# Reordering loads and the first two attention units, with wider idle matmuls, at the start of a fused attention and MLP kernel

## The chip, the cores and the metric

One core of a Trainium2 chip. The metric is the device time of one execution in microseconds (us), smaller is better. "Profile" is one execution recorded by the hardware profiler; its span (first to last instruction) is about 1.7 us shorter than the time.

## The reference

```python
# q, k, v: (8, 8, 576, 64); attention inside chunks of 64 tokens
scores = scale * q_c @ k_c.T ; attn = softmax(scores) ; x = attn @ v_c
x = x.transpose(0, 2, 1, 3).reshape(4608, 512)
h = x @ w_in                                # 512 -> 2048
g = h * sigmoid(beta * h)
out = g @ w_out                             # 2048 -> 512, float32
```

## The kernel before

The 4608 tokens are taken in units of 256, two units making a block of 512. For each unit: scores on TensorE, exp on ScalarE, PV on TensorE, normalisation on VectorE (a reciprocal and a multiply for each half), a transpose of x on TensorE with a copy to SBUF on ScalarE. For each block: sixteen groups "m" of the hidden layer (in the profile `hps`: four matmuls each, then tanh on ScalarE and a multiply on VectorE into `gt`), then the output layer (`ops`). From the third unit on attention is mixed into the matmuls of the MLP. The first two units cannot be: at the start there is nothing else to compute. Idle matmuls on a zeroed tile fill the waits there.

The loads of q, k, v and the weights go through one queue, issued by GpSimd in program order:

```python
# unit 0: half of q, k by SP into raw0, the other half here into qk0[1]
load_v(0)
load_v(1)
load_qk(1)
load_w_in(0)
load_v(2)
load_v(3)
...
for g in range(1, 8):
    load_w_in(g)
# [... w_out, later units ...]
```

and the computation at the start is

```python
emit_idle(10, 512); emit_idle(4, 128)
emit_T_half(0); emit_sc_half(0)          # scores of unit 0, first half of the heads
emit_idle(14, 128)
emit_T_half(1); emit_sc_half(1)
# [... beta ...]
emit_idle(8, 128)
emit_pv(0); emit_norm(0, 0); emit_norm(0, 1)
emit_idle(10, 128); emit_xt_pe(0, 0)
emit_idle(8, 128);  emit_xt_pe(0, 1)
emit_idle(24, 128)
emit_T(1); emit_sc(1, True)              # scores of unit 1
# m0, m1 for the first 256 tokens, PV of unit 1, norms, emit_idle(8, 128), transposes, m2 ... m5 for the first 256,
# then m0 ... m5 for the second 256, then m6 ... m15 for all 512

def emit_idle(n, w):
    d = ps_p.tile([128, 512], FP32, tag="p", name="warm")
    for _ in range(n):
        nc.tensor.matmul(out=d[:, 0:w], lhsT=idle[:, 0:128], rhs=idle[:, 0:w])
```

The softmax here doesn't subtract the row's maximum and nothing guards it: scores larger than these inputs give would overflow.

## Time and profile before

| | before |
|---|---|
| time, median of the 3 runs known ahead | 291.59 us (291.19 to 291.81) |
| TensorE busy | 282.5 us of a span of 290.3 |
| idle matmuls | 86, 9.9 us |
| scores of unit 1 begin | 13.24 us |
| PV of unit 1 begins | 15.56 us |
| first matmul of the output layer (end of block 0's hidden layer) | 31.09 us |

The best single number is the start of the first output-layer matmul: everything of the front lies ahead of it. I call it "first ops" below. It comes from one profiled execution, and that one took 292.08 us.

### The profile page before, as it was taken

How to read it: one execution, taken by the hardware profiler on the slowest of the kernel's cores; microseconds unless marked ns; L12 is line 12 of the kernel's file. 1: busy time of each engine (PE TensorE's matmuls, PEld its weight loads, DVE VectorE, ACT ScalarE, POOL GpSimd, SP SyncE). 2: the span in 40 equal slices, each digit the busy share in tenths (PEclk: the TensorE clock that was granted, in tenths of full speed). 3: DMA queues.
4: the chain of work that ended last, by engine and by line, in shares of the span. 5: the costliest groups of instructions: out<-in, count | busy, mean ns of one | idle time of the engine just before them, and what ended most of it. 6: DMA issues, size and time to landing. Idle time of an engine off the chain costs nothing.

```text
span 290.3 us, 6592 instructions
## 1 busy us (share of the span) xinstructions
PE 282.5 (97%) x2750; PEld 138.6 (48%) x2750; DVE 139.7 (48%) x254; ACT 146.3 (50%) x227; POOL 97.5 (34%) x126
## 2 busy tenths in 40 slices
PE   8799999999999999999999999999999999999995
PEld 4674445545544444444444444444444444444444
DVE  3467444687266544534454444545353636433300
ACT  3288318783556545454544554455445544444411
POOL 8863668479152985070807070000000000000000
PEclk9999999999999999999999999999999999999999
DMA  9999999999969999999999999524343212001011
GB/s 138 174 196 205 180 181 211 210 157 159 129 98 143 171 180 148 194 143 156 125 160 146 158 108 183 114 71 95 87 105 78 74 37 74 36 36 38 36 72 72
DMA packets 141932, 36.86 MB, mean 127 GB/s; under 512 B 130000, under 2 KB 137424, under 8 KB 141904
## 3 DMA queue, kind: packets, MB, share of 16 engines
q0 software_dynamic: 101216, 18.10, 80.8%
q1 hardware_dynamic: 40544, 18.24, 31.1%
q8 instruction: 21, 0.34, 0.5%
q10 hardware_dynamic: 144, 0.13, 0.1%
q14 instruction: 7, 0.06, 0.1%
HBM read 36.71 MB, written 9.44 MB: 159 GB/s over the span
## 4 chain that ended last, share of the span: by engine, by line
PE 90%; DVE 2%; DMA 2%; POOL 2%; ACT 1%; issue 1%; DVEq 0%; POOLq 0%
PE hps L303 43%; PE ops L335 41%; DMA ku<-in_k_dram 2%; PE x L256 2%; PE sc L231 2%; PE sc L218 1%; PE ops L547 1%; DVE x L271 1%; POOL vbig L110 1%; POOL h L360 1%; PE xp L287 1%; ACT xt L288 1%; ACT sg L313 1%; DVE kT L154 0%; DVE qT L154 0%
## 5 line engine op out<-in xcount | busy, mean ns | idle before, releaser
L317 DVE SCALAR_TENSOR_TENSOR gt<-sg,hps 128x512 f16<-128x512 f32 (+1 forms) x154 | 99.3, 652 | 115.0 <-ACT sg L313 114.8
L313 ACT ACTIVATE sg<-hps,beta 128x512 f32<-128x512 f32 (+1 forms) x154 | 100.6, 660 | 73.8 <-PE hps L303 73.8
L303 PE MATMUL hps<-xt,win 128*128 128x512 f16 (+1 forms) x616 | 136.7, 365 | 0.7 <-issue 0.3
L335 PE MATMUL ops<-wout,gt 128*128 128x512 f16 x560 | 131.1, 379 | 0.0
L303 PEld LDWEIGHTS <-win 128*128 128x128 f16 x616 | 58.3, 98 | 61.5 <-issue 1.5
L335 PEld LDWEIGHTS <-gt 128*128 128x128 f16 x560 | 53.7, 98 | 63.3
L345 ACT ACTIVATE osb<-ops 128x512 f32<-128x512 f32 x35 | 20.9, 598 | 44.3 <-PE ops L335 44.3
L110 POOL DMA_DIRECT2D vbig<-in_v_dram x40 | 34.1, 871 | 11.4 <-DMA wout<-in_moe_w_out_dram 4.3
L96 POOL DMA_DIRECT2D qu<-in_q_dram x22 | 18.7, 863 | 39.8 <-DMA qT<-qu 36.4
L271 DVE TENSOR_TENSOR x<-x,rd 128x512 f16<-128x512 f32 (+1 forms) x40 | 25.2, 637 | 1.4
L96 POOL DMA_DIRECT2D ku<-in_k_dram x22 | 18.8, 876 | 0.0
L240 ACT ACTIVATE et<-sc 128x512 f16<-128x512 f32 (+1 forms) x10 | 7.5, 768 | 10.4 <-PE sc L231 10.3
L267 DVE RECIPROCAL rd<-x 128x8 f32<-128x8 f32 x36 | 7.2, 200 | 10.2 <-PE x L256 10.2
L352 PE MATMUL warm<-idle 128*128 128x128 f16 (+1 forms) x86 | 9.9, 272 | 1.2 <-DVE braw L356 1.2
L224 ACT ACTIVATE et<-sc 128x1024 f16<-128x1024 f32 x10 | 10.2, 1016 | 0.0
L256 PEld LDWEIGHTS <-et 64*64 64x64 f16 x576 | 6.3, 107 | 7.5 <-issue 3.0
L288 ACT COPY xt<-xp 128x512 f16<-128x512 f16 x12 | 6.7, 588 | 4.5 <-PE xp L287 4.5
L256 PE MATMUL x<-vbig,et 64*64 64x65 f16 x576 | 8.6, 195 | 0.3 <-DMA vbig<-in_v_dram 0.3
L102 POOL DMA_DIRECT2D qu<-in_q_dram x10 | 7.8, 789 | 2.4 <-DMA win<-in_moe_w_in_dram 1.4
L102 POOL DMA_DIRECT2D ku<-in_k_dram x10 | 7.7, 768 | 2.4 <-DMA win<-in_moe_w_in_dram 1.3
L352 PEld LDWEIGHTS <-idle 128*128 128x128 f16 x86 | 6.0, 105 | 4.1 <-issue 2.8
L154 DVE STREAM_TRANSPOSE kT<-ku 128x512 f32<-128x512 f32 x7 | 5.0, 711 | 4.4 <-DMA ku<-in_k_dram 4.3
(34 smaller groups left out, 57.1 us busy)
## 6 DMA issues: line engine op xcount, KB each, us to landing
out_dram<-osb SPq DMA_DIRECT2D x35, 256.0 KB, 3.8
vbig<-in_v_dram POOLq DMA_DIRECT2D x32, 128.0 KB, 7.6
qu<-in_q_dram POOLq DMA_DIRECT2D x20, 128.0 KB, 5.5
ku<-in_k_dram POOLq DMA_DIRECT2D x20, 128.0 KB, 7.4
win<-in_moe_w_in_dram POOLq DMA_DIRECT2D x8, 256.0 KB, 8.8
wout<-in_moe_w_out_dram POOLq DMA_DIRECT2D x4, 512.0 KB, 12.2
qu<-in_q_dram POOLq DMA_DIRECT2D x4, 256.0 KB, 6.8
ku<-in_k_dram POOLq DMA_DIRECT2D x4, 256.0 KB, 7.2
```

The source lines that it names most:

```text
L96: nc.gpsimd.dma_start(out=tv[off:off + n, sp], in_=src[b, :, s:s + n, :].rearrange("h p d -> p h d"),)
L102: nc.gpsimd.dma_start(out=t[off // 2:(off + n) // 2], in_=src[b, :, s:s + n, :].rearrange("h (p r) d -> p h r d", r=2),)
L110: nc.gpsimd.dma_start(out=vbig[off:off + n, i, :, 0:D], in_=v[b, :, s:s + n, :].rearrange("h p d -> p h d"),)
L224: nc.scalar.activation(out=et, in_=sc, func=ACTF.Exp, scale=scale)
L256: nc.tensor.matmul(out=x[64 * c:64 * c + 64, r, g, 0:D + 1], lhsT=(et[64 * r:64 * r + 64, s, 4 * c + g, :] if u < XU else et[64 * r:64 * r ...
L271: nc.vector.tensor_tensor(out=o, in0=x[:, r, :, 0:D], in1=rd[:, r].to_broadcast(list(o.shape)), op=ALU.mult)
L303: nc.tensor.matmul(out=hps[:, 0:n], lhsT=w_in16[m // 2][:, kk, (m % 2) * 128:(m % 2) * 128 + 128], rhs=xr[:, c0 // CH:(c0 + n) // CH, 2 * ...
L313: nc.scalar.activation(out=sg[:, 0:n], in_=hps[:, 0:n], func=ACTF.Tanh, scale=beta2[:, m:m + 1])
L317: nc.vector.scalar_tensor_tensor(out=gt_t[j][:, m, c0:c0 + n], in0=sg[:, 0:n], scalar=1.0, in1=hps[:, 0:n], op0=ALU.add, op1=ALU.mult,)
L335: nc.tensor.matmul(out=ops, lhsT=gt_t[j][:, kk, t * 128:(t + 1) * 128], rhs=w_out16[kk // 4][:, kk % 4, :], start=(kk == 0), stop=(kk == K ...
L345: nc.scalar.activation(out=osb, in_=ops, func=ACTF.Copy, scale=0.5)
L352: nc.tensor.matmul(out=d[:, 0:w], lhsT=idle[:, 0:128], rhs=idle[:, 0:w])
```

## The change

The intent: have unit 1's scores done early by loading its q and k ahead of all v, all v ahead of w_in, computing unit 1's scores ahead of unit 0's PV, and filling the waits with fewer and wider idle matmuls. The diff is cut at the dots; left out is also a condition in `emit_T` that keeps the next loads behind the new scores.

```diff
-        load_v(0)
-        load_v(1)
         load_qk(1)
-        load_w_in(0)
-        load_v(2)
-        load_v(3)
+        for i in range(4):
+            load_v(i)
...
-        for g in range(1, 8):
+        for g in range(8):
             load_w_in(g)
...
-        emit_idle(10, 512)
-        emit_idle(4, 128)
+        emit_idle(11, 512)
         emit_T_half(0)
         emit_sc_half(0)
-        emit_idle(14, 128)
+        emit_idle(3, 512)
         emit_T_half(1)
         emit_sc_half(1)
...
-        emit_idle(8, 128)
+        emit_idle(13, 512)
+        emit_T(1, ("qT", "kT"))
+        emit_sc(1)
+        loads_to(5)
+        emit_idle(4, 512)
         emit_pv(0)
         emit_norm(0, 0)
         emit_norm(0, 1)
-        emit_idle(10, 128)
+        emit_idle(3, 512)
         emit_xt_pe(0, 0)
-        emit_idle(8, 128)
+        emit_idle(3, 512)
         emit_xt_pe(0, 1)
-        emit_idle(24, 128)
-        emit_T(1)
-        emit_sc(1, True)
+        emit_idle(2, 512)
+        emit_pv(1)
+        emit_norm(1, 0)
+        emit_norm(1, 1)
         a0, v0 = emit_m(0, 0, 0, 256, True)
         a1, v1 = emit_m(0, 1, 0, 256, True)
         a0()
         a1()
-        emit_pv(1)
-        emit_norm(1, 0)
-        emit_norm(1, 1)
-        emit_idle(8, 128)
+        emit_xt_pe(1, 0)
         v0()
         v1()
-        emit_xt_pe(1, 0)
         a0, v0 = emit_m(0, 2, 0, 256, True)
         ... (m3 follows the last transpose; m4 and m5 are no longer split in halves)
```

More of the change, by code (lines that the diff above doesn't have):

```diff
@@ L159, in emit_T @@
             )
-        if "qT" in which and u not in (6, 7, 8):
+        if which[-1] == "qT" and u not in (6, 7, 8):
             loads_to(u + 4)
@@ L407 @@
         a1()
-        emit_pv(1)
-        emit_norm(1, 0)
-        emit_norm(1, 1)
-        emit_idle(8, 128)
+        emit_xt_pe(1, 0)
         v0()
         v1()
-        emit_xt_pe(1, 0)
         a0, v0 = emit_m(0, 2, 0, 256, True)
-        a1, v1 = emit_m(0, 3, 0, 256, True)
         a0()
         emit_xt_pe(1, 1)
-        a1()
         v0()
-        v1()
-        emit_m(0, 4, 0, 256)
-        emit_m(0, 5, 0, 256)
-        for m in range(6):
+        emit_m(0, 3, 0, 256)
+        for m in range(4):
             emit_m(0, m, 256, 256)
-        for m in range(6, KFF):
+        for m in range(4, KFF):
             emit_m(0, m)
```

## The prediction

> **What bounds the kernel now.** I read the page first: the busy table, the slices, then the chain of waits in order of time, the timeline of the first 50 us, and the times from issue to landing of single loads.
>
> ```profile
> span 290.3 us, 6592 instructions
> PE 282.5 (97%) x2750; PEld 138.6 (48%) x2750; DVE 139.7 (48%) x254; ACT 146.3 (50%) x227; POOL 97.5 (34%) x126
> ...
> PE   8799999999999999999999999999999999999995
> ...
> L352 PE MATMUL warm<-idle 128*128 128x128 f16 (+1 forms) x86 | 9.9, 272 | 1.2 <-DVE braw L356 1.2
> ```
>
> TensorE is busy 97% of the span; only the first three slices (about 20 us) have gaps, and 9.9 us of its busy time are idle matmuls, all there. The change touches only that stretch. The chain of waits shows how it is ordered now:
>
> ```profile
> 2.89 1.76 POOL vbig L110 x2
> 4.65 0.96 POOL qu L102
> 5.61 6.25 DMA ku<-in_k_dram
> 11.88 0.71 DVE kT L154
> 12.60 0.60 DVE qT L154
> 13.24 0.53 PE sc L231 x41
> 13.77 0.50 issue
> 14.27 0.38 PE sc L231 x23
> 14.65 0.98 PE hps L303 x8
> 15.63 0.28 PE x L256 x16
> 16.18 0.77 DVE x L271 x2
> ...
> 20.11 10.98 PE hps L303 x60
> 31.09 6.91 PE ops L335 x32
> ```
>
> Read: start, length, what. The second unit's k, issued behind two v loads, lands at 11.86; then both transposes, the scores (with a 0.50 us hole in the middle), PV, normalisation, transposes of x. From 20.11 the first block's hidden layer (hps) runs without a gap to 31.09, and then everything to the end is TensorE back to back. So the change is worth what it does to that 31.09.
>
> The timeline gives the tail of the front, which sets it:
>
> ```profile
> 15.56 0.60 PE L256 MATMUL x<-vbig,et 64*64 64x65 f16 x32
> 15.94 0.21 DVE L267 RECIPROCAL rd<-x 128x8 f32<-128x8 f32 x1 [2.75 <-PE x L256]
> 17.43 0.59 ACT L288 COPY xt<-xp 128x512 f16<-128x512 f16 x1 [0.90 <-PE xp L287]
> 18.64 0.59 ACT L288 COPY xt<-xp 128x512 f16<-128x512 f16 x1 [0.25 <-PE xp L287]
> ```
>
> PV of the second unit starts at 15.56; the last copy of its xt ends at 18.64 + 0.59 = 19.23. Only then can hps use the second half of the block.
>
> **Landings.** Narrow windows of the DMA view give issue start plus time to landing: half of unit 0's k 6.73; v0 2.86 + 4.7 = 7.56; v1 8.96; q(1) 10.41; k(1) 11.81; w_in(0) 6.47 + 7.6 = 14.07; v2 14.6; v3 about 15.5; w_in(1) 9.54 + 7.3 = 16.84; then about 1.35 us per w_in and 2.6 per w_out. Loads land one behind the other; the queue is the pace, not the issue (0.9 us each). The packet records give 1.0 us per v load, 1.48 per q or k load and 1.35 per w_in load, while the engines do nothing else.
>
> [...] the first idle matmuls start 0.43 us apart (1.59, 2.02, 2.45), while a later run of hps takes 1.73 us for eight (0.216 each). [...]
>
> **The change part by part.**
>
> *Idle matmuls.* Before 10 of 512 and 76 of 128, after 39 of 512. Warm, 39 x 0.216 = 8.4 us, with eleven cold about 10.7; before 9.9. No TensorE time is saved; each group is a timer that fills a wait. [...]
>
> *Loads.* Up to v3 nothing is added; w_in(0) moves from before v2 to behind v3. Hence q(1) and k(1) move up by two v loads (2.0 us by packets, 2.2 by landings): q(1) 8.2, k(1) 9.6. v1 takes k(1)'s old place or slightly better, 11.3 to 11.8. v2 and v3 gain w_in(0)'s 1.35: v3 about 14.0. w_in(0) takes v3's place, 15.5. From w_in(1) (16.84) on, the order and the bytes in front are the same, so all later landings stay.
>
> *Unit 1 scores.* The q transpose now goes first, in the shadow of k's landing; k: 9.6 + 0.7 = 10.3. TensorE: scores of unit 0 end at 7.7 as before (they wait for the unchanged first loads); 13 idle take 2.8, to 10.5; scores 10.5 to 11.2 against 13.24 to 14.65 before. The hole of 0.50 seems to be instruction fetch (a fetch packet at 11.94) and should not hit here. So scores finish 3.4 us earlier. One exp of 1.02 instead of two: 11.3 to 12.3.
>
> *Unit 0 PV, now behind them.* 4 idle to 12.05; first half 12.05, second half needs the PSUM that the exp frees, 12.4 to 12.7. Before, this was done by 9.3: 3.4 us later. VectorE: 0.21 + 0.76 each: norms end at 13.4 and 14.3. TensorE: 3 idle 13.35; transposes 13.45 to 13.85; 3 idle 14.5; transposes 14.5 to 14.9; 2 idle 15.33.
>
> *Unit 1 PV.* Its v has long landed (14.0), but in program order it stands behind all this: about 15.35 against 15.56. That is the point: **the chain changes its cause, not its length**. 0.2 us gained.
>
> *Tail.* PV 15.35 to 15.95; VectorE from 15.75, norms end at 16.7 and 17.7. m0 and m1 of the first half 15.95 to 16.85 (w_in(0) 15.5), transposes to 17.25, m2 to 17.7 (w_in(1) 16.84), transposes 17.75 to 18.15, m3 to 18.6. ScalarE: two tanh of 0.42 from 16.5, copy 17.4 to 18.0, tanh to 18.45, last copy 18.45 to 19.05, against 19.23 before. 0.2 gained.
>
> *Bulk.* The second half starts at 19.1 with four groups of 256 done: left 4 x 0.43 + 12 x 0.863 = 12.08, end 31.2. Before six groups had been done when the gapless run began, and its end was 31.09. So the 0.2 gained is given back, because fewer first-half groups fill the wait (m4 and m5 are no longer there, 0.86 us). Sum: 31.2 - 31.09 = **+0.1 us**, with some 0.5 of doubt. Later consumers have room for a small shift either way: k(3) lands at 42.65, its transposes end at 43.97, scores begin at 45.19.
>
> **The rivals.**
> 1. *The gain passes through.* If v3 sets PV of unit 1, it moves from 15.5 to about 14.1: 1.4 us, 290.2. For: before, v3 landed within 0.1 us of that PV. Against: program order and the two norms of unit 0 stand ahead. About 15%.
> 2. *All of the scores' 3.4 us passes through:* 288.2. Against: scores are followed by unit 0's PV and norms, which moved back by as much. Under 3%.
> 3. *A transfer takes the wait's place.* w_in(0) moves back 1.4 us to 15.5, and m0 wants it at 15.95; w_in(1) 16.84 and m2 17.25. With 0.4 us of slack, a later landing would cost up to 0.5 to 1.0: 292.1 to 292.6. v1 at 11.8 against 12.05 is as tight. About 20%.
> 4. *Clock.* [...] The busy share is as high as before; 3%.
>
> **Range and chances.** Median before 291.59, plus 0.1 by the sum. The idle groups look fitted to the arrivals (13 of them end 0.2 us behind k's transpose), which speaks for a form tried on the chip, so I shade 0.3 toward faster: 291.4. Doubts of 0.5 in the sum, 0.3 between runs and the first and third rivals give 290.5 to 292.3. Two per cent is 5.8 us: a gain like that would have to remove over a quarter of the first 20 us, where work after k's landing at 9.6 already takes until 19; a loss like that needs several microseconds of half clock or a lost load. Hence 0.015, 0.965, 0.02.
>
> **What would show it.** In the chain of waits, the DMA of k should shrink to some 5.7 us and end near 9.6; scores of unit 1 near 10.5 without a hole; unit 0's PV behind it, near 12; unit 1's PV near 15.3 with its v landed over a microsecond earlier; the last early copy of xt ends near 19.0; first ops matmul near 31.2. Wrong would be: PV of unit 1 near 14 (rival 1), hps waiting for w_in (rival 3), idle matmuls 0.43 us apart after 8 us (rival 4), or a first ops matmul that moves without the end moving by as much.

The sum came to 31.2 - 31.09 = +0.1 us, on 291.59, shaded to 291.4. "Warm" and "cold" are the two spacings of the idle matmuls in the trace, 0.216 and 0.43 us; the 3% of rival 4 was the author's estimate.

## The result

| | before | after |
|---|---|---|
| median of 6 runs | 291.50 us (291.19 to 291.98) | 291.69 us (291.44 to 292.25) |
| first ops in the profile | 31.09 us | 31.27 us |

The ratio is 1.0007, with a 95% interval of 0.9994 to 1.002. A ratio here is the mean time of one kernel's fast runs over that of the other's in the same rounds, so it is not quite the ratio of the medians. It is the same time within the noise, +0.07%. The page of the changed kernel, head and the row of the idle matmuls:

```profile
span 290.0 us, 6476 instructions
...
L352 PE MATMUL warm<-idle 128*128 128x512 f16 x39 | 11.2, 429 | 1.2 <-DVE braw L356 1.2
```

There are 39 idle matmuls for 86, and 11.2 us of them for 9.9. The chain of waits after (start, length, what), cut to the lines that answer to those of before:

```profile
3.74 6.45 DMA ku<-in_k_dram
...
10.21 0.72 DVE kT L154
...
10.98 0.71 PE sc L231 x64
11.69 0.97 PE warm L352 x4
12.66 0.28 PE x L256 x16
...
14.02 0.40 PE xp L287 x4
14.42 0.65 PE warm L352 x3
15.06 0.22 PE xp L287 x4
15.29 0.43 PE warm L352 x2
15.72 0.38 PE x L256 x31
...
18.36 0.60 ACT xt L288
...
19.00 12.27 PE hps L303 x64
31.27 6.91 PE ops L335 x32
```

The intent was met and gained nothing. Unit 1's k lands at 10.19 instead of 11.86, its scores begin at 10.98 instead of 13.24, without the 0.50 us hole in their middle. But now unit 0's PV (12.66 in this view) and its two transposes stand between those scores and unit 1's PV, which starts at 15.72, against 15.63 in the same view before. The last early copy of xt ends at 18.96 instead of 19.23; but four groups of the first half have been computed when the run of hps without a gap begins, where it had been six, and first ops is 0.18 us later.

The span in this profile is 0.3 us *shorter* than before's although first ops is later. The difference lies at 99 us, where the profile before has one more hole that the one after has not:

```profile
98.99 0.35 issue
```

From first ops to there the two traces keep the shift of +0.17 (90.25 against 90.42 at one long run of hps), and behind it the changed kernel is 0.34 ahead. "issue" is time with no releaser in the profile. The cause of this hole is open. Run 1, with as many TensorE instructions as the kernel before, has one of 0.55 us ahead of the same matmul (the 1271st), and the changed kernel, with fewer instructions, has none there; but both stand 4.2 to 4.5 us behind an instruction fetch, not 2.4 us as the holes of runs 7 and 9 do.

### The profile page after: what moved, and what is told of

Same layout as the page of the kernel before. It is cut to its first block, busy times and chain, and to the rows that moved or that the text cites. A ratio compares the mean times of both kernels' runs of the same rounds, so it can differ in the third digit from the quotient of the medians.

```text
span 290.0 us, 6476 instructions
## 1 busy us (share of the span) xinstructions
PE 283.1 (98%) x2695; PEld 135.5 (47%) x2695; DVE 139.8 (48%) x252; ACT 146.0 (50%) x224; POOL 97.5 (34%) x126
## 4 chain that ended last, share of the span: by engine, by line
PE 91%; DMA 2%; ACT 2%; DVE 2%; POOL 1%; issue 1%; DVEq 0%; ACTq 0%; POOLq 0%
PE hps L303 43%; PE ops L335 41%; DMA ku<-in_k_dram 2%; PE x L256 2%; PE sc L231 2%; PE sc L218 1%; PE ops L540 1%; ACT xt L288 1%; DVE x L271 1%; ACT sg L313 1%; PE warm L352 1%; POOL h L360 1%; PE xp L287 1%; DVE kT L154 0%; ACT osb L345 0%
## 5 line engine op out<-in xcount | busy, mean ns | idle before, releaser
L303 PEld LDWEIGHTS <-win 128*128 128x128 f16 x608 | 57.6, 98 | 61.8 <-issue 0.9
L240 ACT ACTIVATE et<-sc 128x1024 f16<-128x1024 f32 (+1 forms) x9 | 7.4, 834 | 10.2 <-PE sc L231 10.2
L352 PE MATMUL warm<-idle 128*128 128x512 f16 x39 | 11.2, 429 | 1.2 <-DVE braw L356 1.2
```

What stands on the lines that cost most here:

```text
L303: nc.tensor.matmul(out=hps[:, 0:n], lhsT=w_in16[m // 2][:, kk, (m % 2) * 128:(m % 2) * 128 + 128], rhs=xr[:, c0 // CH:(c0 + n) // CH, 2 * ...
```

## The experiments

All gave correct results. Kernels of one call shared a chip and the runs of the kernel before: the first four, the next four and the last four. The kernel before had medians of 291.79, 292.61 and 291.75 in these; on the chip of the second call it scattered from 291.38 to 294.62, so I compare the kernels of that call with each other.

The landing of unit 1's k differs from run to run. Where this shifts everything, I also give the interval from the start of unit 1's scores to first ops: **20.29 us in the changed kernel** (31.27 - 10.98).

### 1. The order of the loads alone

```diff
 # the kernel before, with the changed kernel's loads
+        load_qk(1)
+        for i in range(4): load_v(i)     # then w_in(0..7)
```

> The order of the loads changed, the order of the computation as before. My theory (two orders that must match; the chain is k, scores, PV and norms, in program order): v1 now lands at about 11.8 instead of 9.0, and unit 0's PV stands ahead of unit 1's transposes and scores in program order, so PV of unit 0 starts near 12.0 (9.01 for its second half before), its norms end near 14.0, and VectorE transposes k and q of unit 1 only then; PV of unit 1 near 17.4, first ops matmul near 32.9, time +1.8 us against before (about 293.3). Rival (k's early landing is itself the gain and the order is a detail): scores of unit 1 two us earlier than 13.24 and the time 1 to 2 us shorter.

Measured: median 294.63 of four runs, ratio 1.0099 (1.0051 to 1.0147). First ops at 33.61. PV of unit 0 begins at 11.02 and its second half at 11.87 (expected 12.0), PV of unit 1 at 18.16 (expected 17.4). The excess over the forecast has its own cause: the granted clock was 0.998, 0.994, 0.993 and 0.987 in the four runs, with times of 292.56, 294.84, 294.43 and 296.63. In the profile (clock 0.994) ten idle matmuls of 128 took 1.25 us instead of 0.73 in the timeline, after waits of 2.3 and 0.5 us for v. So the loads' order by itself costs, as the theory said, and in this profile the clock fell on top, behind the wait of 2.3 us (0.92 granted from 10 to 12 us, 0.50 from 12 to 14, 0.73 from 14 to 16).

### 2. The order of the computation alone

```diff
 # the changed kernel, with the loads of the kernel before
-        load_qk(1)
-        for i in range(4): load_v(i)
+        load_v(0); load_v(1); load_qk(1); load_w_in(0); load_v(2); load_v(3)
```

> The order of the computation changed, the loads as before. My theory: k of unit 1 lands at 11.8 as before, q's transpose is done in its shadow, scores of unit 1 start near 12.7, unit 0's PV near 14.3 and unit 1's PV near 17.3, which is 1.7 behind the changed kernel's 15.65; first ops matmul near 32.8, time about 293.2, +1.6 us. Rival (a late v or w_in was what limited the changed kernel): here v1 has landed at 9.0 and w_in(0) at 14.1, so the time would be below the changed kernel's 291.7.

Measured: median 293.88, ratio 1.0077 (1.0051 to 1.0102). The two runs at clock 1.00 took 293.26 and 293.13, the forecast value; two at 0.993 took 294.66 and 294.50. In the profile, one of the latter, unit 1's scores begin at 12.56 (expected 12.7), PV of unit 1 at 18.62 (17.3) and first ops is 34.17. The rival is out: with v and w_in early it should have been faster than the changed kernel.

Loads and order each cost some 2 to 3 us by themselves and much less together (0.7 us, run 10): they are one change, each half moving the wait that the other would leave.

### 3. Two more idle matmuls ahead of unit 1's PV

```diff
-        emit_idle(2, 512)
+        emit_idle(4, 512)
         emit_pv(1)
```

> The changed kernel with four idle matmuls of 512 instead of two just ahead of unit 1's PV: 0.43 us more of TensorE at that place. My theory (that PV is set by TensorE's program order, its v having landed at 14.6, a microsecond earlier): PV of unit 1 at 16.08 instead of 15.65, and first ops matmul 0.3 to 0.45 us later than 31.27. Rival (v's landing, or w_in(0)'s landing at about 16.0, sets it): no more than 0.1 us.

Measured: median 292.57, ratio to before 1.0029 (1.0012 to 1.0045). The changed kernel has 1.0007 and, repeated below, 0.9999, so about 0.002 to 0.003, 0.6 to 0.9 us, came from 0.43 us of idle matmuls; the intervals touch, so this size is loose. PV of unit 1 began at 15.81. First ops in the profile was 31.36, only 0.09 later, but that was the fastest of the six runs and its scores started early, at 10.71; the interval is 20.65, +0.36, all of it between the scores and unit 1's PV (5.10 us against 4.74). Unit 1's PV is set by what stands ahead of it on TensorE, not by a landing.

### 4. No idle matmuls behind the scores

```diff
-        emit_idle(4, 512)
         emit_pv(0)
 ...
-        emit_idle(3, 512)
         emit_xt_pe(0, 0)
-        emit_idle(3, 512)
         emit_xt_pe(0, 1)
-        emit_idle(2, 512)
         emit_pv(1)
```

> The changed kernel without the twelve idle matmuls behind unit 1's scores (4, 3, 3 and 2 of 512); the thirteen ahead of them stay. The chain of waits of the changed kernel counts 0.97 + 0.65 + 0.43 = 2.05 us of idle matmuls. My theory: most of it lies beside work that takes as long. PV of unit 0 can start at 11.8 (v1), its second half only when the exp has ended (12.8), norms end near 14.1, PV of unit 1 near 14.7 where v3 has landed (14.6); but m0 stands behind it and w_in(0) lands near 16.0, so m0 stays at 16.0; first ops matmul 0.1 to 0.5 us earlier, time 291.2 to 291.6. Rival (idle matmuls on the chain are pure cost): first ops matmul 2 us earlier, near 29.3. Second rival (they keep the clock up): matmuls at half speed in the trace, 1 to 2 us slower.

Measured: median 292.19, and six runs that fall into groups by their clock: 290.67 and 291.33 at 1.00; 292.13, 292.26 and 292.71 at 0.994; 293.18 at 0.987. The profile is of the last. Two-microsecond windows: the stretch, its length, busy us and instruction count of TensorE, of its weight loads, of VectorE, ScalarE and GpSimd, then the granted clock, and the load and rate (GB/s) of the DMA engines. First without, then with the idle matmuls:

```profile
12.00:14.00 2.00, 1.11 (x24) 0.66 (x23) 1.53 (x5) 0.93 (x2) 2.00 (x3) 1.00 1.70 183
14.00:16.00 2.00, 1.13 (x38) 0.79 (x37) 1.51 (x6) 0.59 (x1) 1.16 (x3) 0.60 1.45 197
16.00:18.00 2.00, 2.00 (x13) 1.56 (x12) 0.93 (x3) 1.17 (x3) 1.09 (x2) 0.50 1.45 196
```

```profile
12.00:14.00 2.00, 1.90 (x39) 0.74 (x36) 1.00 (x4) 0.78 (x1) 1.29 (x2) 1.00 1.66 192
14.00:16.00 2.00, 1.98 (x45) 1.19 (x45) 0.83 (x3) 1.17 (x2) 1.48 (x2) 1.00 1.46 196
16.00:18.00 2.00, 2.00 (x31) 1.45 (x20) 1.91 (x7) 1.26 (x4) 1.18 (x3) 1.00 1.45 195
```

Without them TensorE is busy for some 1.1 of 2.0 us, and the clock falls to half at 14.4 and stays there until 21.2. PV of unit 1 did start early (14.04) and m0 waited for w_in(0) to 15.38, as the theory has it, but first ops was 32.69. At clock 1.00 the two runs average 291.0, at 0.994 the three average 292.37: one stretch of half clock costs 1.4 us, and it comes in four runs of six. The second rival holds. **The idle matmuls cost up to 2.05 us of the chain and not all of them can go**: they buy the clock (0.987 or 0.994 in four of six runs without them, 0.998 to 1.00 in all twelve of the changed kernel). Not all twelve are needed: run 6 takes three out and moves two, and all its six runs were at clock 1.00. Here the longest gap of TensorE after the scores was 0.9 us, and the clock fell; run 12's profile had one of 1.6 us and kept it. So the longest gap does not part these runs. Nor does the share of busy time in full. Where the clock fell, TensorE had been busy for 59% of the 3.41 us before it (2.03 us here; 40% in run 2 and 23% in run 1; 3.41 us, or twice that, is how long the clock then stayed at half). But the kernel before kept it with 60% in as long a stretch (10.90 to 14.31), and run 12's profile with about 53% (no matmul from 10.59 to its scores at 12.19). Every fall came behind a stretch of low share, and the share alone is not shown to decide.

### 5. Unit 1's PV moved up

```diff
         emit_xt_pe(0, 0)
-        emit_idle(3, 512)
-        emit_xt_pe(0, 1)
-        emit_idle(2, 512)
         emit_pv(1)
         emit_norm(1, 0)
         emit_norm(1, 1)
+        emit_xt_pe(0, 1)
+        emit_idle(2, 512)
+        emit_xt_pe(1, 0)
 ...  # m0 and m1; tanh of m0; emit_xt_pe(1, 1); tanh of m1; other PSUM buffers for these transposes
```

> The changed kernel with unit 1's PV moved up: directly behind the first transposes of x of unit 0, ahead of the second ones (those transposes get other PSUM buffers, so nothing waits for a buffer); unit 1's transposes follow interleaved with m0 and m1; idle groups after the scores 4, 3 and 2. My theory (program order on TensorE, with unit 0's norms on VectorE, sets unit 1's PV; v has landed): its PV starts near 14.45 instead of 15.65, the second half near 14.95 when unit 0's norms free its PSUM, norms of unit 1 end near 16.9 instead of 17.9, last early copy of xt ends near 18.4 instead of 18.96, first ops matmul near 30.6 instead of 31.27, time 0.4 to 0.9 us below the changed kernel's, if the clock stays at 1.00. Rival (v3's landing or the norms' length sets it): first ops matmul within 0.2 of 31.27. New rival after the last runs (the clock): a window of half clock if TensorE is too idle between 11 and 16, 1.4 to 1.7 us slower.

Measured: median 291.70, all clocks 0.999 or 1.00. A miss in time. Unit 1's PV began at 14.75 and its second half at 15.44, behind unit 0's norms (expected 14.45 and 14.95). In this profile (the slowest of six) k landed at 10.70, half a microsecond later than in the changed kernel's. But the tail ate most of the gain, by my own mistake:

```profile
18.30 0.46 ACT xt L288
...
18.78 0.49 ACT sg L313
...
19.29 0.43 DVE gt L317
...
19.77 11.83 PE hps L303 x60
```

The tanh of m1 was queued behind the last copy of xt, so a PSUM buffer that the next group needed came free only at 19.72. The interval is 20.11, 0.18 shorter than the changed kernel's, first ops 31.60. It does not part the theories; the next run brings that PV forward in another way, with a mended tail.

### 6. Split, with fewer idle matmuls ahead of unit 1's PV

Unit 0's PV is split around the idle matmuls; three idle matmuls are taken out, and two move from ahead of unit 1's PV to behind it; unit 1's transposes stand between m0 and m1 with the tanh ahead of the copy. The expectation calls it "as the hoisted one", which it is not: here unit 1's PV stays behind unit 0's second transposes, as in the changed kernel.

```diff
-        emit_idle(4, 512)
-        emit_pv(0)
+        emit_pv(0, (0,))          # first half needs only v and the early exp
+        emit_idle(4, 512)         # fills the wait for unit 1's exp, which frees the PSUM
+        emit_pv(0, (1,))
         emit_norm(0, 0)
         emit_norm(0, 1)
-        emit_idle(3, 512)
         emit_xt_pe(0, 0)
         emit_idle(3, 512)
         emit_xt_pe(0, 1)
-        emit_idle(2, 512)
         emit_pv(1)
         emit_norm(1, 0)
         emit_norm(1, 1)
+        emit_idle(2, 512)
         # m0, tanh; xt_pe(1, 0); m1, tanh; xt_pe(1, 1); ...
```

> A version meant to beat both: as the hoisted one, and unit 0's PV is split around the four idle matmuls, so that its first half starts at v0 and v1's landing (11.8) and not after them (12.6), the idle ones filling the wait for the exp. By my theory: unit 0's norms end near 14.2 instead of 14.9, unit 1's PV near 14.7 and 15.0, its norms near 16.9; m0 goes first, at w_in(0)'s landing (15.4 to 16.0), and four groups of the first half fill TensorE until the last copy of xt near 18.0; first ops matmul 30.1 to 30.6, time 290.6 to 291.1 with the clock at 1.00. If the front is already bound by w_in's landing, it stays above 30.8. If the clock drops, 1.4 us or more is added.

Measured: median 290.72, six runs from 290.63 to 291.17, all at clock 1.00; ratio to before 0.9939 (0.9903 to 0.9976), and 0.33% below the changed kernel's 291.69 median, which is of another call. In this call run 8, which keeps the changed kernel's pace, had 291.92.

```profile
10.97 0.68 PE sc L231 x64
11.65 0.25 PE x L256 x16
11.90 0.97 PE warm L352 x4
12.87 0.25 PE x L256 x16
13.12 0.33 PE xp L287 x4
13.45 0.65 PE warm L352 x3
...
14.52 0.28 PE x L256 x16
...
17.18 12.98 PE hps L303 x72
30.16 6.91 PE ops L335 x32
```

The scores begin at 10.97 as in the changed kernel, and first ops is at 30.16: an interval of 19.19, 1.1 us shorter. Unit 1's PV begins at 14.5 instead of 15.7, behind less, and hps runs without a stop from 17.18. This is the theory's central claim with the load order untouched: what stood in program order between the scores and unit 1's PV held the changed kernel. Run 12 parts the gain.

### 7. Wide idle matmuls alone

```diff
 # the kernel before; groups of 128 become groups of 512 of nearly equal length
-        emit_idle(10, 512); emit_idle(4, 128)     ->  emit_idle(11, 512)
-        emit_idle(14, 128) / (8) / (10)           ->  emit_idle(3, 512) / (2) / (3)
-        emit_idle(8, 128) / (24) / (8)            ->  emit_idle(2, 512) / (6) / (2)
```

> The kernel before with the same idle time in fewer and wider matmuls: groups of 11, 3, 2, 3, 2, 6 and 2 of 512 for 10 of 512 and 4, 14, 8, 10, 8, 24 and 8 of 128. My theory: an equal filler; first ops matmul within 0.3 of 31.09, no difference above 0.2% in time. Rival (wide ones hold the clock better, or block the start of real work longer): a granted clock that differs from before's 0.998 to 1.0, or first ops matmul more than 0.5 off.

Measured: median 291.23 of four runs (290.75 to 291.42), the kernel before 292.61. First ops 30.27, 0.82 earlier than before: not the "equal filler" of the theory. The profile is of the fastest of the four.

```profile
13.13 0.71 PE sc L231 x64
13.84 0.98 PE hps L303 x8
14.81 0.28 PE x L256 x16
...
30.27 6.91 PE ops L335 x32
```

k landed 0.12 earlier; the rest is unit 1's scores, which take 0.71 us in one piece instead of 1.41 with the hole of 0.50 us in their middle. It is gone here. Both traces show instruction fetches as single packets of 16 KB on queue 8 (21 of them before, for 5,500 weight loads and matmuls of TensorE), one starting at 11.94 before and at 12.80 here. Counting weight loads and matmuls of TensorE from its first, the hole before comes after number 446: 364 up to the last idle matmul, then 41 score matmuls with their weight loads. With wide idle matmuls 446 falls into the second half of unit 1's PV: TensorE stops there, within one of that count, for 0.21 us (15.06 to 15.27), but VectorE is still at work on the first half.

### 8. w_in(0) between v1 and v2

```diff
         load_v(0); load_v(1)
+        load_w_in(0)
         load_v(2); load_v(3)
```

> The changed kernel with w_in(0) loaded between v1 and v2 again, as before the change; it moves v2 and v3 back by one w_in load, 1.35 us: v3 from 14.6 to 15.5 to 16.0. My theory gives v3 one microsecond of slack ahead of unit 1's PV at 15.65: that PV moves by 0 to 0.35 us only, first ops matmul 31.3 to 31.6, time as the changed kernel's to 0.4 us more. Rival (v's landing sets that PV in the changed kernel): PV 1.35 later, time 1.3 us more. Second rival (w_in(0)'s landing at about 16.0 was holding m0 and with it the end): time less than the changed kernel's.

Measured: median 291.92. PV of unit 1 in the chain at 15.88, first ops 31.44, both in the forecast; the scores had begun 0.16 later, so the interval is 20.30, that of the changed kernel. Moving v2 and v3 back by a whole w_in load changed nothing: v had that slack, and w_in(0) was not holding the end.

### 9. The changed kernel with narrow idle matmuls

```diff
-        emit_idle(3, 512)   # every group behind the first scores
+        emit_idle(12, 128)  # 13 -> 52, 4 -> 16, 3 -> 12, 3 -> 12, 2 -> 8
```

> The changed kernel with every idle matmul behind the first scores as four of 128 in place of one of 512: the same loads and order, the same idle time within 0.25 us, 84 matmuls (168 TensorE instructions) more. The wide-idle run took 0.8 us off the kernel before by its first ops matmul, and the 0.50 us hole in unit 1's scores was gone from the chain. Theory (TensorE runs into a late instruction fetch after a number of instructions, and the wide groups moved that point out of the chain): here the fetch comes earlier, a hole of 0.3 to 0.6 us without a releaser shows between unit 1's scores and unit 0's PV, first ops matmul near 31.7, time 0.3 to 0.6 us above the changed kernel of this batch. Rival (the gain of the wide ones was only a front that happened to start early in that run): no hole in the chain, within 0.15 us of the changed kernel.

Measured: median 293.21, the changed kernel on the same chip 291.76; ratios to before 1.0041 (1.0020 to 1.0062) and 0.9999. Clock 0.999 or 1.00 in all. The hole came where the theory has it; its cost was above the forecast (1.4 us, not 0.3 to 0.6).

```profile
12.53 0.15 PE x L256 x4
12.69 0.66 issue
13.35 0.31 PE x L256 x12
...
32.03 6.91 PE ops L335 x32
```

A hole of 0.66 us sits in unit 0's PV, and first ops is 0.76 later. Counted the same way, it comes after number 446 again (one more weight load had started): 438 up to the last idle matmul ahead of that PV, then four matmuls with their weight loads. The fetch packet started at 10.89 and the hole ended 2.46 us later; before, it was 11.94 and 2.33 us. The same count to within one in two kernels, much the same delay behind the packet, and no other releaser: I read the hole as a late instruction fetch; the width of the idle matmuls moved where it fell. Most of the other traces fit: in run 5 TensorE stops for 0.23 us at the same count, 2.5 us behind the packet, and where TensorE came to that count 2.8 us or more behind the packet (nine traces) it does not stop there; run 4 came to it 2.46 us behind and shows no stop. The medians differ by 1.4 us, but the profiled runs only by 0.77 (292.52 against 291.75), as first ops does; what makes this kernel's other runs slower, up to 293.88, no trace shows.

### 10 and 11. Wide idle matmuls and the changed kernel again, on one chip

> The kernel before with wide idle matmuls once more, this time beside the changed kernel on one chip. Theory: loads and order cost about 1.0 us and wide idle matmuls give 0.8; so this one is 0.4 to 1.0 us below the changed kernel of this batch, first ops matmul 30.2 to 30.6, clock at 1.00 in every run. Rival (chance of one run): within 0.2 us of the kernel before's undisturbed runs.

> The changed kernel once more, as the measure for this batch: 291.5 to 291.9, first ops matmul 31.0 to 31.6, k of unit 1 landing between 10.2 and 10.8, clock 0.999 or 1.00 in all runs. If it were below wide_idle_again, loads and order would not cost anything.

Measured: wide idle matmuls in the kernel before 291.28 (290.71 to 291.50), ratio 0.9975 (0.9958 to 0.9993), clock 0.999 or 1.00; the changed kernel 291.76 (291.68 to 292.35), ratio 0.9999 (0.9982 to 1.0017). By their means, 291.20 and 291.90, loads and order together cost 0.7 us, inside the forecast range. First ops of the former was 30.84 this time, later than the range: the profile shows hps waiting for a w_in load that landed at 17.04, so in this profile that version is at the pace of the loads. The changed kernel's first ops was 31.27, to the hundredth that of its first profile, with k at 10.18; one of its runs had clock 0.998.

### 12. The split alone

```diff
-        emit_idle(4, 512)
-        emit_pv(0)
+        emit_pv(0, (0,))
+        emit_idle(4, 512)
+        emit_pv(0, (1,))
```

> The changed kernel with unit 0's PV split around the four idle matmuls and nothing else, to part the two edits of the split and hoisted version (290.72, first ops matmul 30.16). Theory: norms of unit 0 start at 12.2 instead of 12.97 and end near 14.2 instead of 14.87; but unit 1's PV still stands behind the second transposes and two idle matmuls: 15.1 instead of 15.65; first ops matmul 30.7 to 30.9, time 0.3 to 0.6 us below the changed kernel of this batch. Rival (the split alone was the gain): first ops matmul near 30.2. Other rival (the hoist alone was): within 0.15 us of the changed kernel.

Measured: median 291.68 (291.15 to 292.69), mean 291.74 against 291.90; the forecast of 0.3 to 0.6 us is missed by half. The profile is of the slowest run; k landed at 11.40 in it, first ops was 32.20. The interval is 20.01, -0.28. So neither the split (-0.28) nor the hoist with its bad tail (-0.18) makes up the 1.1 us of run 6. The chains of waits part it. From unit 1's scores to its PV the changed kernel takes 4.74 us, this run 4.46 and run 6 3.55; from that PV to first ops they take 15.55, 15.55 and 15.64. So all of run 6's gain lies ahead of that PV: 0.28 us by the split, and 0.91 more with five idle matmuls fewer there (1.08 us of the changed kernel's chain); the tail gives nothing. No run takes the five out without the split, so the 0.91 is a difference of two traces.

## Why the prediction was right

The measured median was 291.69 after a forecast of 291.4 in 290.5 to 292.3, and the chances had 0.965 on "within 2%". The unshaded sum (291.59 + 0.1) hit the median to the hundredth, and in first ops the +0.1 was +0.18. So close a hit is luck: k landed 0.6 later than forecast and unit 1's PV began 0.3 later, but from that PV to the last copy of xt it took 3.3 us instead of 3.7; and the profiles end in the other order than first ops, by the hole at 99 us. Point by point:

- **"The chain changes its cause, not its length": shown.** PV of unit 1 moved from 15.56 to 15.65 in the timeline (forecast about 15.35). Run 3 shows that TensorE's order sets it, run 8 that v does not, runs 1 and 2 that loads and order only work together, and run 6 that with less ahead of it 1.1 us goes. Of rivals 1 and 3 nothing is seen: in the changed kernel the view of TensorE's waits from 5 to 32 us lists only the transposes of unit 0 (1.0 us), and no v or w_in load.
- **k's landing, 9.6: 0.6 too early.** It was 10.19. q landed at 8.2 as forecast; k came 2.0 us behind it, where the forecast took the 1.4 us of the kernel before. Why is open. Through this queue 128 KB took 4.4 to 7.7 us and 256 KB 5.2 to 9.8 us from issue to landing in the first 15 us. Over the ten profiles in which q and k of unit 1 are loaded ahead of v, k landed between 9.7 and 11.4; in the four with the loads of the kernel before between 11.6 and 11.9. The forecast took one number, from the early end.
- **Scores without the hole: right, with the cause misplaced.** I put it down to instruction fetch and took it off with the scores' move. Runs 7 and 9 show that the width of the idle matmuls took it away. So "each group is a timer, no time is saved" was right about busy time and wrong about the part: the wide idle matmuls alone bring 0.8 us by the means of run 10's call (0.5 by the medians; 0.8 and 0.25 in first ops of the two profiles), and the new loads and order lose about as much (0.7). The zero is a sum of the two.
- **Rival 4, the clock: did not happen in the changed kernel** (0.998 to 1.00 in all twelve runs), but run 4 lost the clock with no gap above 0.9 us after the scores. The idle matmuls are no mere timers.
- **The tail: right to a tenth.** Last copy 18.96 against 19.05, "fewer first-half groups" as the way in which the gain is given back, first ops 31.27 against 31.2.
- **The shade of 0.3 toward faster was unfounded.** Idle groups fitted to arrivals show that someone tuned the form, not that it gained.

Left open: why the kernel before scattered up to 293.78 at an almost full clock on the chip of the second call; what makes run 9's other runs slower than its profiled one; the hole at 99 us; and why k lands so unevenly in the new order.

## What to carry to other kernels

Loading an input earlier pays only if nothing else in program order stands between it and the step that sets the end: here k landed 1.67 us earlier and the time stayed the same. Follow the chain to that step before counting the wait as a gain. Idle matmuls did three things at once here: they held the clock (without twelve of them it was 0.987 or 0.994 in four runs of six), they took time on the chain (up to 2.05 us), and they counted as instructions, which shifted where a hole fell (0.50 us in unit 1's scores with 86 of them, gone from there with 29 wide ones in run 7; 0.66 us in unit 0's PV with 84 more than the changed kernel in run 9). The 29 wide ones held the clock at 0.998 to 1.00 in the ten runs of 7 and 10. When a change with several parts comes out at zero, run its parts alone: here one part gained and the other lost as much, and the gaining part alone (291.28) or the changed kernel with a split PV and fewer idle matmuls ahead of unit 1's (290.72) beat both kernels, by less than 0.5% each.
